# A new written-out order for five engines' queues, and one tile turned by TensorE instead of a DMA

## The chip, the cores and the metric

The kernel runs on one core of a Trainium2 chip. The metric is the device time of one execution in microseconds (us). Three runs of the kernel before took 1645.88, 1646.5 and 1651.99 us; the median is 1646.5 us. The engines are named as in the profile: PE is TensorE (PEld its weight loads), DVE is VectorE, ACT is ScalarE, POOL is GpSimd, and SP is the queue that does nothing but issue DMAs.

## The reference, cut to what matters

Four blocks with residuals run one after the other on 2048 tokens of width 512: A, B, A, B. Block A walks over 64 segments of 32 tokens, and each segment needs the memory rows that the segment before it wrote, so the 64 steps form a chain. Block B is linear attention: it sums keys times values over all tokens, and only then can any output row be computed.

```python
# A: S=2048, Dm=512, H=32 heads of Dh=128, M=8 memory rows, seg=32
for s in range(n_seg):                       # 64 steps
    h = concatenate([mem, xs], axis=1)       # 8 + 32 rows
    q, k, v = h @ Wq, h @ Wk, h @ Wv
    p = softmax(where(mask, q @ k.T * scale, -1e9))
    o = (p @ v) @ Wo
    mem = o[:, :M, :]                        # the next step's memory
    outs.append(o[:, M:, :])
# B: phi(t) = where(t > 0, t + 1, exp(t)) + 1e-6
kv, z = einsum(phi(k), v), sum(phi(k))
o = (phi(q) @ kv) / (phi(q) @ z + 1e-6) @ wo
# whole
x = x + A(layernorm(x)); x = x + B(layernorm(x))   # twice
```

## The kernel before

**Tiles and steps.** The 2048 tokens are 16 tiles of 128 rows; four steps of A use one tile. `a_layer(layer)` writes the steps `s` of one A block, with `layer` 0 or 1, and `b_in` and `b_out` of the B blocks are woven in between. Each step consists of named stages, and every operation has a key of layer, step, stage and number:

- `kq0`, `kq1`, `v`: products of the step's 32 rows (8 memory rows and 24 fresh rows) with Wk, Wq and Wv, in two halves of the heads each (L2121, L2010).
- `mem0`, `mem1`: attention of the memory rows, which the next step needs. `x`: attention of the fresh rows.
- `out`: the product with Wo (L2345) into a PSUM bank; half of it is copied to `outW`, then the DVE adds both halves into `y_sb` (L2354). `y_sb` has one slot for all steps' rows, and another for the rows named next.
- `next`: picks the memory rows out of `y_sb` by a product with `selm_sb` (L2371) and copies them into `hT`, the transposed input of the next step's `kq` and `v`.
- `res`: moves the step's other rows from `y_sb` to `dx_sb` by two DMAs, one issued by POOL and one by SP (L1909). Only when both have read `y_sb` can the next step's `out` write it.
- `left0`, `left1`, `leftv` (`left_block`): since 8 rows of a step's 32 tokens are left over, those of four steps are collected and projected together, once for each tile, by 24 groups of four matmuls with 512 columns. `prep` comes before it.
- `prep` (`prepare`): layer norm of the next tile (L2058 to L2064), then the normalised rows are transposed and copied into `hT`. For the first tile of a layer the transpose is a product on PE (L2075) into PSUM; for all others it is a DMA transpose issued by SP (`turn`, L2049) into `xT`. `xT` shares its memory with `vtmp`, which `leftv` also uses.
- `xl` loads a tile of x; in layer 1 `bo` (`b_out`) loads it from `xs_scratch` and corrects it with the B block of layer 0.
- `bi` (`b_in`): the B block's layer norm, a DMA transpose, products and running sums for one tile; it also stores x to `xs_scratch` and phi(q) to `pq_scratch`.
- At the end of layer 1: `lr` projects the last left-over rows of tile 15 and moves them by three DMAs on POOL and three on SP; `ldpq` turns all phi(q) back from `pq_scratch` by four DMA transposes on SP into the space of Wq; `ldxs` loads x; then `bi` of the last tile, `bm` (which folds kv into the output weights) and `bl`, the last B block's output tile by tile.

**What sets the order.** Nothing is scheduled at run time. The dictionary `PLACE` (L16 to L1526) gives every operation of the 1509 stages a number, in the thousandths of a microsecond in which a planner once counted. `schedule` sorts all operations by it, and this order is each engine's instruction stream; the letter `a` or `v` behind a number puts a copy on ACT or on DVE where both can do it. `finalize` adds the semaphore waits that the data need. So the numbers set only who stands behind whom in a queue: an engine that waits for a semaphore holds up all that stands behind it. The costs and latencies that `add` is given (`0.45`, `lat=3.0`) were the planner's inputs; they do not reach the chip.

**The beginning.** SP issues the loads of Wk, Wq and Wv (4 MB each), of Wo in 16 pieces and of `wqkv`, in this order, and stands still while their queue is full; the first DMA transpose comes behind them. `spin4` is a block of products of ones that keeps PE busy until Wq is there.

Of the kernel before, what the change touches and what calls it, by code (L numbers as in the profile page):

```python
# [16 lines left out]
    (0, -9, 'setup'): '1131 3371 2811 2813 9533 9534 10942 10946 10947 11056 11059 15131 15691 15692 17375 17376 19002 27477 29851 31623 38758 39985 10941 570 1130 1690 2250 2810 3370 3930 9531 9532 10940 10943 10944 10948 10949 11055 11058 11060 11061 11062 11210 11770 12330 12890 13450 14010 14570 15130 15690 17372 17371 16250 16810 17370 19001 29419a 9535 10945a 67899 17930 19000 27045 29422 32312 15133 2812 11057',  # L17
    (0, -4, 'start'): '14570v',
    (0, -2, 'left0'): '24454 24886 25965 26396 27036a 28340 28987a 29421',
    (0, -2, 'left1'): '27907 28986 29418 29850 30489a 31621 31858a 32719',  # L20
    (0, -2, 'leftv'): '34490 34922 35353 35785 36425a 37193 37636 37637a 38186 38757',
    (0, -2, 'prep'): '10138 10860 11054 12330 13451 15132 15690v 16250v 30982a 42475a 34099v',
    (0, -2, 'spin4'): '19003',
    (0, 0, 'kq0'): '25533 27044 27476 28555 29854v 32311 29853a 31622',
    (0, 0, 'kq1'): '16810 17373 17374 17377 25317 27036 28339 30489 26397v 27036 31128a 31857',
    (0, 0, 'mem0'): '31992 32718 33289 33090 33557 37080 38186 38756 38913 39315',
    (0, 0, 'mem1'): '33081 33139 34235 33557 37429 39075 39986 40103 40161 40563',
    (0, 0, 'next'): '46847 47346 47347a',
    (0, 0, 'out'): '39707 40323 42290 42396 42399 42400 42476 42477 43826v 45469',
    (0, 0, 'ql'): '29420a 32310a',  # L30
    (0, 0, 'v'): '36217 36648 37192 37636 38263a 39708a',
    (0, 0, 'x'): '33859 34234 34581 34996 35785 37080 36649v 37192v 39075v 36648v 40820 39984 40043 42397 42475 47348a 46705v 39925 40102 42291 42475 55641v 55958a',
    (0, 0, 'xl'): '0',
    (0, 1, 'kq0'): '48093 48944 50705 50706 51332a 51764 51116a 52052',
    (0, 1, 'kq1'): '47446 49173 50708 50709 48525 50707 50899 51115 52685a 53058 52627a 52628',
    (0, 1, 'mem0'): '52626 52684 53056 53175 53324 54186 54407 54808 54274 55148',
    (0, 1, 'mem1'): '53324 53424 53916 54274 54185 54809 55049 55426 54810 56136',
    (0, 1, 'next'): '58338 58392 58657a',
    (0, 1, 'out'): '55640 55698 55958 56135 56353 56571 56790 57089 57718a 57894',
    (0, 1, 'ql'): '47708v 38756v',  # L40
    (0, 1, 'res'): '66656 61715',
    (0, 1, 'v'): '51331 51763 52194 53057 53917v 53424a',
    (0, 1, 'x'): '54391 54811 55147 55639 56571 56702 56948v 56571v 57229a 57088v 57228 57658 57835 57893 58011 58338v 58908v 57717 57776 57952 58123 66655v 62145v',
    (0, 2, 'kq0'): '58907 59338 59770 60417 61714a 62350 61713v 61929',
    (0, 2, 'kq1'): '60202 61497 61712 62144 60849 61065 61281 61928 62713v 63814 62851a 63321',
    (0, 2, 'left0'): '42530 42962 43393 43825 44465a 45106 45584a 46226',
    (0, 2, 'left1'): '44465 44688 45584 45983 46704a 47345 48093a 48525',
    (0, 2, 'leftv'): '45469 46706 47349 47708 48943a 49584 50063 50062a 50704 51763',
    (0, 2, 'mem0'): '62792 63713 64246 64354 64353 64946 65215 65586 65238 65826',
# [2672 lines left out]
```

## Time and profile before

| what | value |
|---|---|
| median of three runs | 1646.5 us |
| profiled execution | 1649.09 us, span from first to last instruction 1647.0 us |
| PE busy | 1544.7 us (94%), 48837 matmuls |
| DVE, ACT, POOL busy | 1219.7, 1056.1, 191.5 us |
| mean granted clock of PE | 0.991 |
| DMA | 58.28 MB |

The span is what the instruction records cover, and the profiled execution has 2.1 us around it. A matmul here covers a quarter of the array's columns (128 rows by 32 columns); four of them run side by side, so a line with a duration of 0.39 us and x4 does not mean that PE is occupied for 0.39 us: the next such group starts about 0.22 us later. In a timeline the columns are the start in us, the duration in us, the engine, the line, the operation, the tiles written and read, and in brackets the engine's idle time before it with what ended it.

### The profile page before, as it was taken

To read this page: it belongs to the slowest core of one execution; us is meant where nothing else is said; L and a number is where in the kernel's file an instruction comes from. 1 tells how busy PE (TensorE), PEld (TensorE's weight loads), DVE (VectorE), ACT (ScalarE), POOL (GpSimd) and SP (SyncE) were. 2 spreads that over 40 slices of the span, in tenths; PEclk is the share of its full clock that TensorE was granted. 3 is DMA by queue.
4 is the path that set the end of the run, shared out by engine and by line. 5 is a ranking of instruction groups with operands and counts; after the bars stand their busy time and mean duration, and the time that the engine had idled before them with its cause. 6 is when DMAs were issued, how large, how long until landed. Compare 5 with 4: busy or idle time off the path is not lost.

```text
span 1647.0 us, 97785 instructions
## 1 busy us (share of the span) xinstructions
PE 1544.7 (94%) x48837; PEld 820.7 (50%) x40483; DVE 1219.7 (74%) x3603; ACT 1056.1 (64%) x3097; POOL 191.5 (12%) x388
## 2 busy tenths in 40 slices
PE   5799999999999998999899999999999999999987
PEld 1345545555555554554444555455555545555543
DVE  3477767777787787777677787777877777777757
ACT  2466667676766666666466675766666666766654
POOL 2011101111111101111100111011111011111010
PEclk9999999999999999999999999999999999999998
DMA  9300001001010001000000100101010111010133
GB/s 380 99 20 19 13 18 23 23 23 22 20 23 14 23 23 22 20 20 23 22 10 16 29 20 19 26 23 26 20 29 13 22 29 26 20 23 19 29 65 104
DMA packets 79892, 58.28 MB, mean 35 GB/s; under 512 B 59416, under 2 KB 74168, under 8 KB 77944
## 3 DMA queue, kind: packets, MB, share of 16 engines
q1 hardware_dynamic: 66456, 36.43, 8.5%
q0 software_dynamic: 12864, 15.46, 3.4%
q8 instruction: 351, 5.75, 1.5%
q14 instruction: 61, 0.50, 0.1%
q10 hardware_dynamic: 160, 0.14, 0.0%
HBM read 25.57 MB, written 10.35 MB: 22 GB/s over the span
## 4 chain that ended last, share of the span: by engine, by line
PE 73%; DVE 10%; DMA 8%; ACT 5%; issue 3%; SPq 1%; POOL 0%; DVEq 0%; POOLq 0%; ACTq 0%
PE pb L2121 26%; PE pb L2010 19%; PE pb L2345 14%; PE pb L2022 8%; DMA arena_sb<-arena_sb 3%; DVE arena_sb L1894 2%; ACT arena_sb L1893 2%; DMA dx_sb<-y_sb 2%; PE pb L2512 2%; DMA Wq_sb<-in_A_Wq_dram 1%; PE pb L2209 1%; DVE arena_sb L2139 1%; DVE st_sb L2058 1%; PE pb L2371 1%; DVE y_sb L2354 1%
## 5 line engine op out<-in xcount | busy, mean ns | idle before, releaser
L1893 ACT ACTIVATE arena_sb<-pb 128x512 bf16<-128x512 f32 (+3 forms) x1039 | 503.8, 511 | 300.9 <-PE pb L2010 154.7
L1894 DVE CAST arena_sb<-pb 128x512 bf16<-128x512 f32 (+3 forms) x600 | 316.9, 535 | 93.0 <-PE pb L2010 47.0
L2121 PE MATMUL pb<-Wk_sb,arena_sb 128*32 128x512 bf16 x4096 | 368.5, 381 | 5.0 <-DMA Wk_sb<-in_A_Wk_dram 2.1
L2345 PE MATMUL pb<-Wo_sb,arena_sb 128*32 128x256 bf16 x10368 | 341.5, 273 | 12.4 <-issue 8.6
L2139 DVE STREAM_TRANSPOSE arena_sb<-arena_sb 128x256 f32<-128x256 f32 x640 | 262.7, 430 | 63.7 <-ACT arena_sb L1893 58.0
L2345 PEld LDWEIGHTS pb<-Wo_sb,arena_sb 128*32 128x32 bf16 x10368 | 258.2, 96 | 56.2 <-issue 20.8
L2121 PE MATMUL pb<-Wq_sb,arena_sb 128*32 128x512 bf16 x3072 | 273.1, 382 | 11.0 <-DVE arena_sb L1894 8.4
L2022 PE MATMUL pb<-arena_sb 128*32 128x128 bf16 (+2 forms) x10800 | 264.0, 208 | 13.1 <-DVE arena_sb L1894 5.1
L1909 POOL DMA_DIRECT2D dx_sb<-y_sb x252 | 128.1, 512 | 1207.5 <-DVE y_sb L2354 829.1
L2121 PE MATMUL pb<-Wv_sb,arena_sb 128*32 128x512 bf16 x2560 | 255.5, 381 | 1.3 <-issue 1.2
L2010 PE MATMUL pb<-Wv_sb,arena_sb 128*32 128x512 bf16 x2560 | 254.9, 381 | 0.0
L2022 PEld LDWEIGHTS pb<-arena_sb 128*32 128x32 bf16 x10800 | 183.9, 95 | 136.1 <-DVE arena_sb L1894 36.9
L2121 PEld LDWEIGHTS pb<-Wk_sb,arena_sb 128*32 128x32 bf16 x4096 | 113.1, 97 | 185.0 <-issue 96.1
L2010 PE MATMUL pb<-Wq_sb,arena_sb 128*32 128x512 bf16 x2048 | 202.9, 380 | 0.0
L1893 ACT ACTIVATE arena_sb<-arena_sb 32x256 bf16<-32x256 bf16 (+2 forms) x396 | 141.2, 359 | 45.9 <-DVE arena_sb L2293 30.1
L2121 PEld LDWEIGHTS pb<-Wq_sb,arena_sb 128*32 128x32 bf16 x3072 | 86.4, 97 | 117.9 <-issue 50.3
L1894 DVE COPY arena_sb<-arena_sb 32x256 bf16<-32x256 bf16 (+2 forms) x522 | 103.1, 201 | 23.5 <-DMA arena_sb<-arena_sb 12.8
L2354 DVE TENSOR_TENSOR y_sb<-pb,outW_sb 64x256 bf16<-64x256 f32 x162 | 67.8, 419 | 65.0 <-ACT outW_sb L1893 52.7
L2257 DVE TENSOR_TENSOR arena_sb<-pb,arena_sb 128x128 bf16<-128x128 f32 x252 | 73.1, 290 | 54.2 <-ACT arena_sb L2245 22.4
L2010 PE MATMUL pb<-Wk_sb,arena_sb 128*32 128x512 bf16 x1024 | 104.1, 384 | 0.4 <-issue 0.4
L2121 PEld LDWEIGHTS pb<-Wv_sb,arena_sb 128*32 128x32 bf16 x2560 | 71.7, 96 | 65.5 <-issue 39.4
L1893 ACT ACTIVATE outW_sb<-pb 64x256 f32<-64x256 f32 x134 | 50.6, 377 | 82.5 <-PE pb L2345 78.8
(111 smaller groups left out, 1800.2 us busy)
## 6 DMA issues: line engine op xcount, KB each, us to landing
Wk_sb<-in_A_Wk_dram SPq DMA_DIRECT2D x1, 4096.0 KB, 13.3
Wq_sb<-in_A_Wq_dram SPq DMA_DIRECT2D x1, 4096.0 KB, 24.6
Wv_sb<-in_A_Wv_dram SPq DMA_DIRECT2D x1, 4096.0 KB, 34.1
Wo_sb<-in_A_Wo_dram SPq DMA_DIRECT2D x16, 256.0 KB, 7.2
xs_scratch<-x_sb POOLq DMA_DIRECT2D x32, 128.0 KB, 2.0
pq_scratch<-arena_sb POOLq DMA_DIRECT2D x31, 128.0 KB, 2.4
x_sb<-xs_scratch POOLq DMA_DIRECT2D x16, 128.0 KB, 2.9
dx_sb<-y_sb SPq DMA_DIRECT2D x126, 12.0 KB
```

Source lines behind the costliest of these rows:

```text
L1893: return e.activation(o() if callable(o) else o, i() if callable(i) else i, ACTF.Copy)
L1894: return e.tensor_copy(o() if callable(o) else o, i() if callable(i) else i)
L1909: add(eng, lambda e: e.dma_start(o, i), 0.55 if eng == "pool" else 0.4, reads=reads, writes=writes, dsem="%s%d" % (kind, k), lat=lat + (0. ...
L2010: return pe.add_instruction(mybir.InstMatmult(name=nc.get_next_instruction_name(), engine=mybir.EngineType.PE, ins=[pe.lower_ap(x), pe.low ...
L2022: r = pe.matmul(o[q], w[:, q], x, start=start, stop=stop, skip_group_check=True, tile_position=(0, 32 * j))
L2058: add("dve", lambda v: v.bn_stats(st[:, 0:6], x), c_dve(512), reads=[xk], writes=[("st", k)])
L2121: r = pe.matmul(o, blk[:, c, :], w, start=(c == 0), stop=(c == 3), tile_position=(0, 32 * j))
L2139: add("dve", lambda v: v.transpose(dst, src(img[:, k, :].bitcast(F32))), 0.445, reads=[("img", k)], writes=[dkey])
L2257: add("dve", lambda v: v.tensor_tensor(oTb[:, s % NO, 16 * b:16 * b + 16, 0:8].rearrange("p (i j) q -> p j i q", i=4), heads(pv.f32()[:, 0 ...
L2345: r = pe.matmul(tl.f32()[32 * j:32 * j + 32, 0:256], oT[:, 4 * hh + n, :], Wo_sb[:, 8 * n + hh, 256 * d:256 * d + 256], start=(hh == 0 and ...
L2354: add("dve", lambda e: e.tensor_tensor(y_sb[0:64, k, :], tl.f32()[a, 0:256], outW[c, v, :], ALU.add), c_dve(256), reads=[("outW", w)], til ...
L2512: r = pe.matmul(dst.f32()[q, :], xlnT[:, c, q], wqkv_sb[:, c, o:o + D], start=c == 0, stop=c == 3, skip_group_check=True, tile_position=(0 ...
```

## The change

All 1509 entries of `PLACE` get new numbers, so that the order of all five queues changes. Of the 2730 operations that can run on ACT or DVE, 580 go from DVE to ACT and 578 from ACT to DVE. The planner's inputs for DMAs are others (they do not reach the chip). In layer 0 the second tile (`G` = 1) is transposed by PE, as the first already was, and not by a DMA; its copies into `hT` read PSUM in place of `xT`.

```diff
 PLACE = {
...
-    (0, 0, 'out'): '39707 40323 42290 42396 42399 42400 42476 42477 43826v 45469',
-    (0, 0, 'next'): '46847 47346 47347a',
-    (0, 1, 'kq0'): '48093 48944 50705 50706 51332a 51764 51116a 52052',
-    (0, 2, 'left0'): '42530 42962 43393 43825 44465a 45106 45584a 46226',
-    (0, 2, 'left1'): '44465 44688 45584 45983 46704a 47345 48093a 48525',
-    (0, 2, 'leftv'): '45469 46706 47349 47708 48943a 49584 50063 50062a 50704 51763',
-    (0, 2, 'prep'): '9530 10939 13450 15134 26396 40323 42289v 46847v 47815v 42398a 42395v',
-    (1, 63, 'lr'): '1509542 1511104 1511279 1511497 1511716 1511934 1512211 1513000 1513332a 1513775 1516848 1516846 1516214 1516213 1515880 1516847 1520274',
-    (1, 63, 'res'): '1517060 1518203',
-    (1, 64, 'out'): '1517329 1517547 1517766 1517984 1518202 1518421 1518639 1518858 1519284a 1519798',
-    (1, 64, 'ldpq'): '1513124',
-    (1, 65, 'ldpq'): '1516273',
-    (1, 66, 'ldpq'): '1516786',
-    (1, 67, 'ldpq'): '1516845',
...
+    (0, 0, 'out'): '44931 44932 45137 45347 46599 46818 47370 47588 48015a 48443',
+    (0, 0, 'next'): '48918 48972 49238v',
+    (0, 1, 'kq0'): '50187 50188 50343 50775 52071v 53366 51639a 52502',
+    (0, 2, 'left0'): '32789 33221 38204 38917 40575a 41216 41694v 43407',
+    (0, 2, 'left1'): '31826 32258 37097 41696 44067v 45136 45626a 47588',
+    (0, 2, 'leftv'): '41218 45139 45624 46168 47588v 49345 49823 51206a 51206 51854',
+    (0, 2, 'prep'): '10030 10753 10947 11280 11535 12011 14073a 14074a 15580a 31272a 14072a',
+    (1, 63, 'lr'): '1516941 1519098 1519098 1519757 1519976 1520458 1521060 1521816 1522467a 1523228 1526143 1526276 1525536 1528233 1524158 1526119 1529184',
+    (1, 63, 'res'): '1526277 1528232',
+    (1, 64, 'out'): '1526275 1526493 1526712 1526930 1527149 1527367 1527585 1527804 1528231v 1528708',
+    (1, 64, 'ldpq'): '1524572',
+    (1, 65, 'ldpq'): '1537336',
+    (1, 66, 'ldpq'): '1538732',
+    (1, 67, 'ldpq'): '1539078',
...
 }
...
     qk_view = [W.rearrange("(c p) h e -> p c (h e)", p=128) for W in (A_Wq, A_Wk, A_Wv)]
 
     def x_move(o, i, k, reads, writes, kind, eng="pool", lat=2.0):
-        add(eng, lambda e: e.dma_start(o, i), 0.55 if eng == "pool" else 0.4, reads=reads, writes=writes,
+        add(eng, lambda e: e.dma_start(o, i), 0.55 if eng == "pool" else 0.66, reads=reads, writes=writes,
             dsem="%s%d" % (kind, k), lat=lat + (0.4 if eng == "pool" else 0.0))
 
     shift = [0]
...
 
     ln_no = [0]
 
-    def turn(o, i, reads, writes, kind, lat=3.0):
-        add("sp", lambda e: e.dma_start_transpose(o, i), 0.45, reads=reads, writes=writes, dsem=kind, lat=lat)
+    def turn(o, i, reads, writes, kind, lat=2.8):
+        add("sp", lambda e: e.dma_start_transpose(o, i), 1.2, reads=reads, writes=writes, dsem=kind, lat=lat)
 
     def layernorm(t, after=None, dst=None):
         k = ln_no[0] % 2
...
             busy = spin(layer, step, "spin", *SPIN[layer, 1]) if not first and G == 0 else None
             at(step, "prep")
             r2 = G % 2
-            tl = layernorm(G, busy, None if G == 0 else (xT, ["vtmp"], "dtx"))
+            pe_turn = G <= first
+            tl = layernorm(G, busy, None if pe_turn else (xT, ["vtmp"], "dtx"))
             if first and G == 0:
                 ready.append(spin(layer, step, "spin4", *SPIN[0, 4]))
                 ready[0].sync.add(late[0])
                 at(step, "prep")
                 P.count = 6
-            if G:
+            if not pe_turn:
                 view = xT.rearrange("p c (g x) -> p c g x", g=4)
                 src, tls, rd, sb, rate = lambda: view, [], ["vtmp"], 1, 4
             else:
...
                 b_out(1, s, t, 0)
             elif t:
                 at(s, "xl")
-                x_move(x_sb[:, slot(t), :], x_view[t], slot(t), [], [("x", slot(t))], "dxl", lat=8.5 if t == 1 else 2.0)
+                x_move(x_sb[:, slot(t), :], x_view[t], slot(t), [], [("x", slot(t))], "dxl", lat=8.5 if t == 1 else 3.0)
 
         at(-4, "start")
         evac(hT[:, 0, 0, :, 0:8], memT0_sb[:, :, :], 32, reads=["memT0"], writes=[("hTm", 0, 0)])
...
                 P.at(1, step + i // 4, "ld" + nm)
                 nd = add("sp", (lambda e, vw=vw, i=i, n=n: e.dma_start(XE[:, 1, i:i + n, :], vw[i:i + n].rearrange("t p d -> p t d")))
                          if w else (lambda e, vw=vw, i=i, n=n: e.dma_start_transpose(
-                             XQ[:, :, i:i + n, :].rearrange("p c t x -> p c (t x)"), vw[i:i + n].rearrange("t p d -> (t p) d"))), 0.6,
+                             XQ[:, :, i:i + n, :].rearrange("p c t x -> p c (t x)"), vw[i:i + n].rearrange("t p d -> (t p) d"))), 0.6 if w else 2.6,
                     reads=[(nm, t) for t in range(i, i + n)], writes=[("XE", w, t) for t in range(i, i + n)],
                     after=P.res["Wq"][1] + free, dsem="dl%s%d" % (nm, i), lat=t0 + 0.22 * i)
                 if prev is not None:
...
             else:
                 e, ek = quarters(e_sb), ["e"]
         else:
-            x_move(x, xs_view[t], k, [("xs", t)], [xk], "dxl")
+            x_move(x, xs_view[t], k, [("xs", t)], [xk], "dxl", lat=2.5)
             turn(e, pq_view[t], [("pq", t)], ek, "dtq")
         td, ty = P.tile(), P.tile()
```

2990 rows, old and new, of the table PLACE are left out of this document.

## The prediction

> **What bounds the kernel now.** I read the page first, then a table of stretches, then the waits of PE.
>
> ```profile
> span 1647.0 us, 97785 instructions
> PE 1544.7 (94%) x48837; PEld 820.7 (50%) x40483; DVE 1219.7 (74%) x3603; ACT 1056.1 (64%) x3097; POOL 191.5 (12%) x388
> ...
> PE 73%; DVE 10%; DMA 8%; ACT 5%; issue 3%; SPq 1%; POOL 0%; DVEq 0%; POOLq 0%; ACTq 0%
> ```
>
> ```profile
> 0.00:62.00 62.00, 36.77 (x665) 9.95 (x415) 18.40 (x57) 14.89 (x41) 10.92 (x42) 0.89 0.82 306
> 62.00:1600.00 1538.00, 1477.43 (x47452) 797.26 (x39404) 1171.77 (x3489) 1020.53 (x3019) 180.04 (x345) 1.00 0.10 22
> 1600.00:1647.00 47.00, 30.45 (x732) 13.45 (x664) 29.54 (x57) 20.65 (x38) 0.55 (x1) 0.88 0.37 112
> ```
>
> In the stretches the columns are the stretch, its length, the busy time of PE, PEld, DVE, ACT and POOL, the clock granted to PE, the DMA share and GB/s. PE is the bound, and the change takes no product away, so it can win only PE's idle time and the time lost at a low clock. The idle time is 62.0 - 36.8 = 25.2 us in the first 62 us, 1538.0 - 1477.4 = 60.6 us in the 1538 us that follow (4%), and 47.0 - 30.5 = 16.5 us in the last 47 us. Both ends also have a mean clock under 1. Per us the ends are the poor stretches, so I look at them by instruction and at the middle by its waits.
>
> ```profile
> PE pb L2121 <- DVE arena_sb L1894: 10.1, 9, 4.0
> PE pb L2345 <- issue: 8.6, 18, 1.0
> ...
> PE pb L2022 <- DVE y_sb L2354: 7.8, 4, 6.4
> ...
> PE pb L2371 <- DVE y_sb L2354: 6.3, 13, 2.6
> ...
> PE pb L2022 <- issue: 2.4, 5, 1.1
> ```
>
> Each row says which instruction of PE waited for whom: us in total, how often, and the longest. Two of the longest, 4.0 and 6.4 us, are single events, one at each end.
>
> **The beginning: tile 2 turned by PE.** Here are the queue of SP, the DVE, and PE.
>
> ```profile
> 2.42 39.21 SPq L1924 DMA_DIRECT2D Wo_sb<-in_A_Wo_dram  x16
> ...
> 42.40 23.53 SPq L2049 DMA_TRANSPOSE arena_sb<-arena_sb  x2
> ```
>
> ```profile
> 12.97 0.56 DVE L2064 TENSOR_SCALAR arena_sb<-x_sb,st_sb 128x512 bf16<-128x512 bf16 x1
> ...
> 52.40 0.29 DVE L1894 COPY arena_sb<-arena_sb 128x128 bf16<-128x128 bf16 x2 [6.90 <-DMA arena_sb<-arena_sb]
> 52.72 0.43 DVE L1894 COPY outW_sb<-pb 64x256 f32<-64x256 f32 x1
> ...
> 57.40 0.42 DVE L2354 TENSOR_TENSOR y_sb<-pb,outW_sb 64x256 bf16<-64x256 f32 x1
> ```
>
> ```profile
> 11.50 0.62 PE L2075 MATMUL pb<-id_sb,arena_sb 128*32 128x128 bf16 x16 [8.34 <-DVE arena_sb L2064]
> 14.18 1.90 PE L2121 MATMUL pb<-Wk_sb,arena_sb 128*32 128x512 bf16 x16 [2.06 <-DMA Wk_sb<-in_A_Wk_dram]
> ...
> 33.52 0.21 PE L2217 MATMUL pb<-arena_sb 128*32 128x64 bf16 x4 [1.28 <-DVE arena_sb L2139]
> ...
> 36.40 0.64 PE L2010 MATMUL pb<-Wv_sb,arena_sb 128*32 128x512 bf16 x4
> 36.83 0.64 PE L2121 MATMUL pb<-Wv_sb,arena_sb 128*32 128x512 bf16 x4
> ...
> 47.98 0.62 PE L2345 MATMUL pb<-Wo_sb,arena_sb 128*32 128x256 bf16 x16 [1.65 <-DMA Wo_sb<-in_A_Wo_dram]
> 52.65 0.62 PE L2121 MATMUL pb<-Wq_sb,arena_sb 128*32 128x512 bf16 x4 [4.05 <-DVE arena_sb L1894]
> ...
> 59.06 0.38 PE L2121 MATMUL pb<-Wq_sb,arena_sb 128*32 128x512 bf16 x4
> 59.28 0.38 PE L2010 MATMUL pb<-Wk_sb,arena_sb 128*32 128x512 bf16 x4
> ...
> 60.50 0.40 PE L2121 MATMUL pb<-Wk_sb,arena_sb 128*32 128x512 bf16 x4
> ```
>
> Tile 2's normalised rows are ready at 12.97 + 0.56 = 13.53 us, but their DMA transpose stands behind the sixteen Wo loads and is issued at 42.40 us; it lands at 52.4 us. Until then PE stands still for 4.05 us with `left0` at the head of its queue. What that holds up matters more: the copy to `outW` of step 0's output stands behind the waiting copies on the DVE and starts at 52.72 us although the product ended at 47.98 + 0.62 = 48.60 us; `y` follows at 57.40 us, and step 1's first `kq` product begins at 60.50 us.
>
> With the change the transpose costs the product of 16 matmuls once, 0.62 us by the row at 11.50 us. It comes ahead of the Wk product, which waits 2.06 us for its weights anyway. The rows are ready at 13.53 us, before Wk's 14.18 us, so I cost it at 0 (0.62 us if that cover is gone). The 24 groups of `left_block` then stand between 31.8 and 47.6 in the new order, ahead of `next` of step 0. They need 24 x 0.22 = 5.2 us, 0.22 us being the spacing from 59.06 to 59.28 us.
>
> ```profile
> 26.00:48.00 22.00, 16.56 (x372) 6.02 (x283) 8.07 (x27) 9.18 (x26) 0.00 (x0) 0.84 1.06 379
> ```
>
> Of these 22 us PE is idle for 5.4 us, and some 3.4 us more go to the low clock (a mean of 0.84, so 0.16 x 22), so 5.2 us of work fit. Step 0's `out` still ends at 48.6 us, when the last piece of Wo has come. From there the copy (0.43), the sum (0.42), the select and its copy (about 0.2 each) and four hand-overs lead to step 1's `kq` at some 50.2 us rather than 60.50 us: -10.3 us. The other end is the removed wait alone, -4.05 us, if the left block doesn't fit before; a loss is excluded, as no transfer is added and the rows are early. I take -9.5, close to the first end, since the queue behind the wait is seen to move with it.
>
> The low clock is a part of this. At 36.40 and 36.83 us the groups come 0.43 us apart, twice the 0.22 us, and the longest wait in the rows just before is 1.28 us. So short waits suffice for a slow stretch, one can stay in the new beginning, and I don't take the whole 10.3 us. The Trainium skill ("TensorE: Matmul & The Clock Gate", Part 1) has the clock halved only after an idle window of some 3.4 us. By that rule no slow stretch is left once the 4.05 us wait is gone, and the term is the whole -10.3; the stretch at 36.40 us doesn't agree with it.
>
> **The end: SP's queue.** The rows are those of SP, DVE and PE.
>
> ```profile
> 1595.31 7.39 SPq L2614 DMA_TRANSPOSE Wq_sb<-pq_scratch  x3
> 1602.74 2.10 SPq L1909 DMA_DIRECT2D dx_sb<-y_sb  x3
> ```
>
> ```profile
> 1597.19 0.42 DVE L2354 TENSOR_TENSOR y_sb<-pb,outW_sb 64x256 bf16<-64x256 f32 x1
> 1606.10 0.42 DVE L2354 TENSOR_TENSOR y_sb<-pb,outW_sb 64x256 bf16<-64x256 f32 x1 [8.50 <-DMA dx_sb<-y_sb]
> ```
>
> ```profile
> 1598.21 1.93 PE L2345 MATMUL pb<-Wo_sb,arena_sb 128*32 128x256 bf16 x64 [0.23 <-ACT arena_sb L1893]
> 1606.58 0.62 PE L2022 MATMUL pb<-y_sb,selz_sb 128*32 128x256 bf16 x8 [6.44 <-DVE y_sb L2354]
> ```
>
> ```profile
> dx_sb<-y_sb POOLq DMA_DIRECT2D x126, 12.0 KB, 1.9
> ```
>
> Step 63's `y` is ready at 1597.6 us, yet SP is issuing three DMA transposes for 7.39 us, and the row moves come behind them. The last step's sum can't write `y_sb` until they have read it: 1606.10 us, with PE idle for 6.44 us. In the old `PLACE` three of the four `ldpq` (1516273 to 1516845) stand ahead of `res` of step 63 (1518203); in the new one it is one (1524572 ahead of 1528232), and the other three stand behind at 1537336 to 1539078. So the move can be issued near 1598 us and lands 1.9 us later, at about 1600, when the last `out` ends too (1598.21 + 1.93 = 1600.14). With the copy, the sum comes at about 1600.6 us: -5.5 us. The three transposes that are moved back then run from 1600 to 1607.4 us on SP. Their first use is in `bl`, after the B block's own chain of some 12 us, so they are covered; if not, up to 5 us come back. I take -5.5, with -7 (a warm clock behind it) and -0.5 as ends.
>
> **The middle.** No wait here is long, and the numbers show no place, only kinds. Waits for "issue" in the two rows above make 8.6 + 2.4 = 11.0 us. The change says it orders by instruction fetches and transfer times. The Trainium skill ("Runtime: NRT & Kernel Launch", Instruction fetch mechanics) holds that fetches are mostly hidden; by that rule this term is 0 and the total 4 us higher. The 18 waits of L2345, up to 1.0 us, speak against it, though no row names the fetch as their cause. `next` waiting for `y` (6.3 us in 13) partly starts here, where the DVE stands before a tile's statistics:
>
> ```profile
> 213.57 0.69 DVE L2058 BATCH_NORM_STATS2 st_sb<-x_sb 128x6 f32<-128x512 bf16 x1 [3.79 <-DMA x_sb<-in_A_x_dram]
> ```
>
> ```profile
> L1893 ACT ACTIVATE arena_sb<-pb 128x512 bf16<-128x512 f32 (+3 forms) x1039 | 503.8, 511 | 300.9 <-PE pb L2010 154.7
> L1894 DVE CAST arena_sb<-pb 128x512 bf16<-128x512 f32 (+3 forms) x600 | 316.9, 535 | 93.0 <-PE pb L2010 47.0
> ```
>
> The copies that change engines (580 one way, 578 the other, 511 against 535 ns) leave both loads as they are: 0. A new order may take away the 11.0 and 6.3 us and the 6.1 us that the first wait row has besides the beginning's 4.0, together some 23 us. It may as well add as much, because it reshuffles every queue and any copy that comes later than planned stops PE. Between -23 and +23 I take -5, a third of the issue waits and a fifth of the `next` waits.
>
> **Sum.** -9.5 - 5.5 - 5 = -20 us. The profiled execution took 1649.1 us (span 1647.0 and 2.1 around it), 2.6 above the median of 1646.5; the same 20 us off the median give **1626.5 us**. What a measurement can tell from no change is about 0.5%, or 8.2 us, hence faster means under 1638.3 and slower over 1654.7.
>
> **The rivals.**
> - *The middle gains its full 23 us.* Then it is 1646.5 - 15 - 23 = 1608.5. For it speaks that DMA is 8% of the chain; against it that the many waits are each under 1 us and come from copies, whose costs the change leaves alone. Chance 0.17.
> - *Only waits are exchanged at the ends.* The left block doesn't fit before the Wo wait (-4) and the moved transposes hold up `bl` (-0.5): with the middle at -5, 1637. Chance 0.08.
> - *The middle gives the ends' gain back.* New waits of about 15 us: 1646.5. It is the case if the new order fits the engines no better than the old one. Chance 0.15.
> - *Slower: SP's queue holds the row moves elsewhere.* In the new order six of the 126 `res` moves on SP stand behind a tile's transpose that was behind them before (those of steps 9, 59 and 60 of layer 0 and 14, 25 and 38 of layer 1; eleven go the other way). If that transpose waits for its own input, the move waits too and the next `y` can't be written, as at the end, where it cost 6.44 us. Six times that is 39 us: 1626.5 + 39 = 1665. It decides only once the hold is longer than the slack, and a step takes 1538 / 126 = 12.2 us, of which the move needs 1.9. A transpose that is itself only a few us late does nothing. Chance 0.10.
>
> **How the numbers follow.** The forecast has 0.50. Faster takes in the forecast, the full gain, the exchange (1637), and a little of the fourth case: 0.50 + 0.17 + 0.08 + 0.02 = 0.77. The rest of the middle's giving back is no change, 0.13; slower is 0.10. The range leaves out the slower case and the far half of the full gain: 1607 to 1650.
>
> **What would show it.** Right: PE's transpose L2075 twice by 13 us; step 1's `kq` at 50 to 51 us; no wait of 4 us for L1894 there; at the end one wait under 2 us for L2354 ahead of L2022, with the three `ldpq` behind the row moves; the middle's idle time at 50 to 60 us. Wrong: PE's idle time in the middle above 75 us, DVE waiting over 10 us for `dx_sb<-y_sb` between the ends, or `left0` of tile 2 again waiting for a DMA.

## The result, and the profile after

The changed kernel takes 1626.1 us in the median of four runs (1621.9 to 1630.0), beside 1648.3 us for the kernel before (its three runs and a fourth): a ratio of 0.9863, with a 95% interval from 0.9829 to 0.9897. The whole interval lies beyond the bound of 0.5%, so it is faster, by 22 us; 20 us and 1626.5 us were forecast.

The page, two lines of it, and then the same three kinds of stretch as before (length, busy time of PE, PEld, DVE, ACT and POOL, granted clock, DMA share, GB/s). The last two rows are cut where the new last step begins.

```profile
span 1627.4 us, 97760 instructions
PE 1534.2 (94%) x48853; PEld 810.1 (50%) x40499; DVE 1226.8 (75%) x3601; ACT 1059.4 (65%) x3099; POOL 191.6 (12%) x388
```

```profile
0.00:62.00 62.00, 41.67 (x1017) 15.51 (x707) 30.09 (x88) 19.70 (x58) 11.43 (x43) 1.00 0.83 306
62.00:1590.00 1528.00, 1464.50 (x47120) 781.35 (x39128) 1166.56 (x3457) 1019.57 (x3005) 179.65 (x344) 1.00 0.10 22
1590.00:1628.00 38.00, 28.02 (x724) 13.25 (x664) 30.14 (x58) 20.15 (x36) 0.55 (x1) 0.92 0.59 151
```

PE's work is the same (16 matmuls more, those of the new transpose), but the first 62 us now hold 41.67 us of it instead of 36.77, and their clock is 1.00 instead of 0.89. PE's idle time in the middle has not fallen: it is 1528.0 - 1464.5 = 63.5 us, where it was 60.6. Here are the waits of PE by kind:

```profile
PE pb L2513 <- DMA arena_sb<-arena_sb: 14.4, 13, 1.9
PE pb L2022 <- DVE arena_sb L1894: 10.0, 28, 1.3
...
PE pb L2372 <- DVE y_sb L2355: 6.1, 20, 0.8
...
PE pb L2121 <- DVE arena_sb L1894: 4.0, 7, 1.3
...
PE pb L2346 <- issue: 3.3, 7, 1.4
PE pb L2022 <- DVE y_sb L2355: 3.3, 3, 1.4
...
PE pb L2022 <- issue: 0.9, 2, 0.6
```

Lines from about 2170 on have moved by one: L2346 is the `out` product, L2355 the sum into `y_sb`, L2372 `next`, L2513 the products of `b_in`. Both long single waits are gone (4.0 at L2121, 6.4 at L2022), and the waits for issue in the two rows quoted before fell from 11.0 to 4.2 us.

The timeline of PE at the beginning, and the DVE's sum in it:

```profile
9.64 0.61 PE L2075 MATMUL pb<-id_sb,arena_sb 128*32 128x128 bf16 x16 [2.40 <-DVE arena_sb L2064]
...
14.55 1.90 PE L2121 MATMUL pb<-Wk_sb,arena_sb 128*32 128x512 bf16 x16 [4.29 <-DMA Wk_sb<-in_A_Wk_dram]
...
36.40 0.39 PE L2121 MATMUL pb<-Wv_sb,arena_sb 128*32 128x512 bf16 x4
36.62 0.39 PE L2010 MATMUL pb<-Wv_sb,arena_sb 128*32 128x512 bf16 x4
...
47.49 0.62 PE L2346 MATMUL pb<-Wo_sb,arena_sb 128*32 128x256 bf16 x16
...
49.04 0.22 PE L2372 MATMUL pb<-selm_sb,y_sb 128*32 128x16 bf16 x8 [0.82 <-DVE y_sb L2355]
49.59 0.40 PE L2121 MATMUL pb<-Wk_sb,arena_sb 128*32 128x512 bf16 x4 [0.33 <-DVE arena_sb L1894]
```

```profile
48.57 0.42 DVE L2355 TENSOR_TENSOR y_sb<-pb,outW_sb 64x256 bf16<-64x256 f32 x1 [0.46 <-ACT outW_sb L1893]
```

The second transpose on PE is done at 10.3 us, in the wait for Wk. Step 0's sum comes 0.5 us after its product instead of 9 us after it, and step 1's `kq` starts at 49.59 us instead of 60.50. At 36.40 us the groups now stand 0.22 us apart, at full clock.

The end: the queue of SP, the DVE, PE.

```profile
1579.63 2.13 SPq L2615 DMA_TRANSPOSE Wq_sb<-pq_scratch  x1
1581.81 6.62 SPq L1909 DMA_DIRECT2D dx_sb<-y_sb  x5
1588.47 6.61 SPq L2615 DMA_TRANSPOSE Wq_sb<-pq_scratch  x3
```

```profile
1590.48 0.42 DVE L2355 TENSOR_TENSOR y_sb<-pb,outW_sb 64x256 bf16<-64x256 f32 x1 [0.47 <-DMA dx_sb<-y_sb]
```

```profile
1587.60 1.93 PE L2346 MATMUL pb<-Wo_sb,arena_sb 128*32 128x256 bf16 x64 [0.39 <-ACT arena_sb L1893]
1590.96 0.40 PE L2022 MATMUL pb<-y_sb,selz_sb 128*32 128x256 bf16 x8 [1.43 <-DVE y_sb L2355]
1591.40 2.55 PE L2010 MATMUL pb<-one_sb 128*32 128x512 bf16 x44
```

The three transposes stand behind the row moves, and the wait for the last sum is 1.43 us instead of 6.44. For the experiments I cut each span at two products that every version has: the start of step 1's first `kq`, and the start of the last `out`.

| profiled execution | start | middle (PE idle in it) | end | span |
|---|---|---|---|---|
| before | 60.5 | 1537.7 (60.6) | 48.8 | 1647.0 |
| after | 49.6 | 1538.0 (64.1) | 39.8 | 1627.4 |
| after, a second job | 50.1 | 1530.9 (58.6) | 39.7 | 1620.7 |

The two ends gave 10.9 + 9.0 = 19.9 us. The medians differ by 22.2 us, so some 2 us are left for the middle; in the second job the ratio was 0.9869 (21.5 us), the ends gave 19.5 us, and 2 us are left again. The intervals reach 4 to 6 us to either side, so these 2 us can't be told from none, nor from the 5 that were forecast. The 7 us between the two middles are a difference of two executions of one kernel. So the middle of one profile is good to about 7 us; the starts of these two agree to 0.5 us and the ends to 0.1.

### The profile page after: what moved, and what is told of

It reads as the page before. It is cut to its first block, busy times and chain, and to the rows that moved or that the text cites. A ratio compares the mean times of both kernels' runs of the same rounds, so it can differ in the third digit from the quotient of the medians.

```text
span 1627.4 us, 97760 instructions
## 1 busy us (share of the span) xinstructions
PE 1534.2 (94%) x48853; PEld 810.1 (50%) x40499; DVE 1226.8 (75%) x3601; ACT 1059.4 (65%) x3099; POOL 191.6 (12%) x388
## 3 DMA queue, kind: packets, MB, share of 16 engines
q8 instruction: 350, 5.73, 1.5%
## 4 chain that ended last, share of the span: by engine, by line
PE 68%; DVE 13%; DMA 10%; ACT 7%; issue 2%; POOL 0%; SPq 0%; DVEq 0%
PE pb L2121 25%; PE pb L2010 17%; PE pb L2346 12%; PE pb L2022 8%; DMA arena_sb<-arena_sb 5%; DVE arena_sb L1894 3%; ACT arena_sb L1893 2%; DMA dx_sb<-y_sb 2%; DMA Wv_sb<-in_A_Wv_dram 2%; DVE arena_sb L2139 2%; PE pb L2513 2%; PE pb L2210 1%; DVE y_sb L2355 1%; DVE arena_sb L2294 1%; PE pb L2372 1%
## 5 line engine op out<-in xcount | busy, mean ns | idle before, releaser
L1893 ACT ACTIVATE arena_sb<-pb 128x512 bf16<-128x512 f32 (+4 forms) x1032 | 499.6, 511 | 293.1 <-PE pb L2010 131.5
L1894 DVE CAST arena_sb<-pb 128x512 bf16<-128x512 f32 (+3 forms) x614 | 322.3, 533 | 105.7 <-PE pb L2010 64.9
L2121 PE MATMUL pb<-Wk_sb,arena_sb 128*32 128x512 bf16 x4096 | 363.3, 381 | 8.2 <-DMA Wk_sb<-in_A_Wk_dram 4.3
L2346 PE MATMUL pb<-Wo_sb,arena_sb 128*32 128x256 bf16 x10368 | 340.0, 273 | 5.7 <-issue 3.3
L2346 PEld LDWEIGHTS pb<-Wo_sb,arena_sb 128*32 128x32 bf16 x10368 | 257.7, 96 | 53.5 <-issue 15.9
L2022 PE MATMUL pb<-arena_sb 128*32 128x128 bf16 (+2 forms) x10800 | 266.6, 209 | 18.3 <-DVE arena_sb L1894 10.0
L2121 PE MATMUL pb<-Wq_sb,arena_sb 128*32 128x512 bf16 x3072 | 266.9, 379 | 3.3 <-DVE arena_sb L1894 2.8
L2022 PEld LDWEIGHTS pb<-arena_sb 128*32 128x32 bf16 x10800 | 183.5, 96 | 149.5 <-DVE arena_sb L1894 45.5
L2121 PE MATMUL pb<-Wv_sb,arena_sb 128*32 128x512 bf16 x2560 | 251.4, 378 | 2.3 <-ACT arena_sb L1893 1.2
L2010 PE MATMUL pb<-Wv_sb,arena_sb 128*32 128x512 bf16 x2560 | 251.2, 378 | 0.0
L2121 PEld LDWEIGHTS pb<-Wk_sb,arena_sb 128*32 128x32 bf16 x4096 | 110.5, 97 | 196.4 <-issue 97.3
L2010 PE MATMUL pb<-Wq_sb,arena_sb 128*32 128x512 bf16 x2048 | 200.7, 379 | 0.0
L1893 ACT ACTIVATE arena_sb<-arena_sb 32x256 bf16<-32x256 bf16 (+2 forms) x411 | 146.9, 361 | 38.8 <-DVE arena_sb L2294 29.1
L2121 PEld LDWEIGHTS pb<-Wq_sb,arena_sb 128*32 128x32 bf16 x3072 | 83.8, 96 | 93.6 <-issue 43.6
L2355 DVE TENSOR_TENSOR y_sb<-pb,outW_sb 64x256 bf16<-64x256 f32 x162 | 67.8, 419 | 55.4 <-ACT outW_sb L1893 51.3
L2121 PEld LDWEIGHTS pb<-Wv_sb,arena_sb 128*32 128x32 bf16 x2560 | 70.1, 95 | 66.1 <-issue 36.9
L2010 PE MATMUL pb<-Wk_sb,arena_sb 128*32 128x512 bf16 x1024 | 101.6, 379 | 0.0
```

Of the source, the lines that this page charges most:

```text
L1893: return e.activation(o() if callable(o) else o, i() if callable(i) else i, ACTF.Copy)
L1894: return e.tensor_copy(o() if callable(o) else o, i() if callable(i) else i)
L2010: return pe.add_instruction(mybir.InstMatmult(name=nc.get_next_instruction_name(), engine=mybir.EngineType.PE, ins=[pe.lower_ap(x), pe.low ...
L2022: r = pe.matmul(o[q], w[:, q], x, start=start, stop=stop, skip_group_check=True, tile_position=(0, 32 * j))
L2121: r = pe.matmul(o, blk[:, c, :], w, start=(c == 0), stop=(c == 3), tile_position=(0, 32 * j))
L2346: r = pe.matmul(tl.f32()[32 * j:32 * j + 32, 0:256], oT[:, 4 * hh + n, :], Wo_sb[:, 8 * n + hh, 256 * d:256 * d + 256], start=(hh == 0 and ...
```

## The experiments

In all of them the ratio is that to the kernel before in the same job, and "us less" is 1 minus the ratio, times the median before.

**1. The product alone.** The old order, and tile 2 transposed on PE; only this entry of `PLACE` differs.

```diff
-    (0, 2, 'prep'): '9530 10939 13450 15134 26396 40323 42289v 46847v 47815v 42398a 42395v',
+    (0, 2, 'prep'): '9530 10939 13450 15134 15500 15690 16805v 16806v 16807v 16808a 16809a',
...
-            tl = layernorm(G, busy, None if G == 0 else (xT, ["vtmp"], "dtx"))
+            pe_turn = G <= first
+            tl = layernorm(G, busy, None if pe_turn else (xT, ["vtmp"], "dtx"))
...
-            if G:
+            if not pe_turn:
```

> The kernel before with one thing changed: tile 2 is transposed by PE, its copies follow at once, and all else keeps the old order (left0 behind step 0's attention). Theory (the two ends carry the whole gain, the product itself most of the beginning's): PE no longer waits 4.05 us for L1894, step 1's kq begins near 53 us instead of 60.5 (the 5.2 us of the left block still come after 46 us), one slow-clock stretch is gone, and the time falls by 6 to 8 us to about 0.996 of before. Rival (the order carries the beginning): the wait is only exchanged for the one on Wo and y, kq at 56 us or later, -2 to -4 us, ratio 0.998.

Measured: 1632.4 us, ratio 0.9917 (0.9903 to 0.9932), 14 us less. `kq` of step 1 started at 53.2 us (-7.3), the end stayed at 48.6 us, and the middle of this execution was 8.0 us shorter. The first groups of the left block, before and in this run:

```profile
53.05 0.64 PE L2010 MATMUL pb<-Wk_sb,arena_sb 128*32 128x512 bf16 x4
53.47 0.64 PE L2121 MATMUL pb<-Wq_sb,arena_sb 128*32 128x512 bf16 x4
```

```profile
48.28 0.39 PE L2121 MATMUL pb<-Wq_sb,arena_sb 128*32 128x512 bf16 x4
48.49 0.39 PE L2010 MATMUL pb<-Wk_sb,arena_sb 128*32 128x512 bf16 x4
```

The 7.3 us are the wait and the slow clock behind it. Before, the left block started 4.67 us after the last part of `out`, and its first 14 groups came 0.43 us apart; here it starts 0.45 us after it, with groups some 0.22 us apart from the first on. From there to `kq` it was 7.85 us before and is 4.95 here. SP and PE at the end of this run:

```profile
1580.04 7.01 SPq L2615 DMA_TRANSPOSE Wq_sb<-pq_scratch  x3
1587.09 2.10 SPq L1909 DMA_DIRECT2D dx_sb<-y_sb  x3
```

```profile
1590.95 0.61 PE L2022 MATMUL pb<-y_sb,selz_sb 128*32 128x256 bf16 x8 [6.09 <-DVE y_sb L2355]
```

So the product gives most of the beginning without the new order, and leaves the end's wait as it was. The 8 us in the middle were not expected (the forecast was 6 to 8 us in all). With them PE's waits for issue fell from 14.9 us in 31 to 8.3 in 18, although the order is the old one; runs 5 to 9 come back to this.

**2. The DMA transpose back, in the new order.** The changed kernel, with tile 2 turned by a DMA again, and its copies and left block near their old places (`leftv` 1.5 us later). So this run undoes the product and the new place of the left block together.

```diff
-    (0, 2, 'left0'): '32789 33221 38204 38917 40575a 41216 41694v 43407',
-    (0, 2, 'left1'): '31826 32258 37097 41696 44067v 45136 45626a 47588',
-    (0, 2, 'leftv'): '41218 45139 45624 46168 47588v 49345 49823 51206a 51206 51854',
+    (0, 2, 'left0'): '42530 42962 43393 43825 44465a 45106 45584a 46226',
+    (0, 2, 'left1'): '44465 44688 45584 45983 46704a 47345 48093a 48525',
+    (0, 2, 'leftv'): '46969 48206 48849 49208 50443a 51084 51563 51562a 52204 53263',
...
-    (0, 2, 'prep'): '10030 10753 10947 11280 11535 12011 14073a 14074a 15580a 31272a 14072a',
+    (0, 2, 'prep'): '10030 10753 10947 11280 11535 42400 42500v 46847v 47815v 42510a 42505v',
...
-            pe_turn = G <= first
+            pe_turn = G == 0
```

> The changed kernel with tile 2 transposed by a DMA again, and its left block back at the old numbers (leftv 1.5 later, as the banks need it); all else is the new order. Theory: the DMA again lands at 52 us behind the weights, PE waits some 4 us, kq of step 1 at 59 to 61 us instead of 49.6, and the time is 9 to 11 us over the changed kernel's (ratio to before about 0.993). Rival (the new order absorbs a late tile): kq at 53 us or earlier, +3 us.

Measured: 1638.5 us, ratio 0.9966 (0.995 to 0.9983). PE's timeline:

```profile
47.52 0.62 PE L2121 MATMUL pb<-Wq_sb,arena_sb 128*32 128x512 bf16 x4 [6.10 <-DVE arena_sb L1894]
...
58.53 0.40 PE L2121 MATMUL pb<-Wk_sb,arena_sb 128*32 128x512 bf16 x4
```

The wait for the DMA's copies is back (6.10 us), `kq` starts 8.9 us later than after, and the end keeps its gain (40.6 us). From here to the changed kernel are 0.0097 to 0.0103, 16 to 17 us, more than the 9 to 11 expected: 9 us of them are the beginning, the rest lies in the middle (1544.3 us here, in an execution 6.6 us over this kernel's median), where one profile is only good to some 7.

**3. The transposes in front of the row moves, in the new order.** The other half undone. The moves of step 63 and of the last rows are put behind the last transpose, and the sum behind them (their entries `lr` and `out` are not shown).

```diff
-    (1, 63, 'res'): '1526277 1528232',
+    (1, 63, 'res'): '1526277 1528800',
...
-    (1, 65, 'ldpq'): '1537336',
+    (1, 65, 'ldpq'): '1526000',
-    (1, 66, 'ldpq'): '1538732',
+    (1, 66, 'ldpq'): '1526001',
-    (1, 67, 'ldpq'): '1539078',
+    (1, 67, 'ldpq'): '1528750',
```

> The changed kernel with the loads of phi(q) put back ahead of the last row moves on SP (two ahead of lr's moves, the third ahead of step 63's). Theory: y of the last step waits for the move again, PE idle 5 to 6.5 us ahead of L2022 with selz, the clock falls behind it, and the end (from the last out to the end of the span) goes from 39.8 us back towards 48.8 us: +6 to +9 us. Rival (the transposes are needed early and the wait is covered by bl): +0 to +2 us.

Measured: 1625.5 us, ratio 0.9876 (0.986 to 0.9892). PE at the end:

```profile
1585.90 0.62 PE L2022 MATMUL pb<-y_sb,selz_sb 128*32 128x256 bf16 x8 [6.64 <-DVE y_sb L2355]
...
1586.72 3.67 PE L2010 MATMUL pb<-one_sb 128*32 128x512 bf16 x44
```

By the profile the mechanism is there: the wait is 6.64 us again, and the stretch from the last `out` to the end is 45.1 us, 5.3 more than after. The total does not show it: 6 to 9 us more than the changed kernel were expected, and the interval holds the changed kernel's ratios (0.9863, 0.9869). This execution's middle was short (1527.6 us), 10.5 and 3.4 us under the two of the changed kernel; why, this run doesn't show. Run 4 tests the same three transposes in the old order, where the total does show them.

**4. Both small edits in the old order.** Run 1, with three more entries changed:

```diff
-    (1, 65, 'ldpq'): '1516273',
+    (1, 65, 'ldpq'): '1518269',
-    (1, 66, 'ldpq'): '1516786',
+    (1, 66, 'ldpq'): '1518270',
-    (1, 67, 'ldpq'): '1516845',
+    (1, 67, 'ldpq'): '1518271',
```

> The kernel before with two things changed: the product of e1, and three of the four phi(q) loads moved on SP behind step 63's row move. 1500 numbers stay old. Theory (the middle gives nothing): -14 to -18 us, ratio about 0.990, and the stretch from step 1's kq to the last out stays at 1537.7 us. Rival (the middle's new order is worth 5 us or more, hidden by the spread of the profiled run): e4 stays 5 us or more over the changed kernel's time after the difference at the beginning is taken off.

Measured: 1625.1 us, ratio 0.987 (0.9852 to 0.9888), 21 us less. Against run 1 that is 7.7 us, and its end is 41.1 us where run 1's is 48.6: total and profile agree on the three transposes. Four entries of `PLACE` and the switch of `pe_turn` come out at the ratio of 1509 new entries, though not by the same way: against the kernel before, the beginning is 6.2 us shorter here and the end 7.6 (13.9 in all, where the changed kernel has 19.9), and the other 7 us lie in this execution's middle (1527.8 us), under the old order. PE's timeline, and the stretch from 26 to 48 us of this kernel:

```profile
33.36 0.21 PE L2218 MATMUL pb<-arena_sb 128*32 128x64 bf16 x4 [1.28 <-DVE arena_sb L2139]
...
36.50 0.65 PE L2010 MATMUL pb<-Wv_sb,arena_sb 128*32 128x512 bf16 x4
36.93 0.65 PE L2121 MATMUL pb<-Wv_sb,arena_sb 128*32 128x512 bf16 x4
...
47.96 0.62 PE L2346 MATMUL pb<-Wo_sb,arena_sb 128*32 128x256 bf16 x16 [1.54 <-DMA Wo_sb<-in_A_Wo_dram]
...
1584.89 0.40 PE L2022 MATMUL pb<-y_sb,selz_sb 128*32 128x256 bf16 x8 [0.93 <-DVE y_sb L2355]
```

```profile
26.00:48.00 22.00, 16.50 (x372) 5.96 (x280) 8.06 (x27) 9.33 (x27) 0.00 (x0) 0.84 1.06 378
```

Here the slow stretch at 36.50 us is left and part of the left block still stands behind Wo, so `kq` starts at 54.3 us. The new order's own gain at the beginning is the difference to its 49.6 us, 4.7 us (3.6 against run 1's 53.2 us, with the same beginning).

**5 and 6. The same orders with 32 more weight loads.** One number of `spin4`'s products changes: 32 of its products load their weights anew. They lie in PE's wait for Wq and cost no time there; all of PE's instructions behind them move by 32 places. Run 5 does it to the kernel before, run 6 to the changed one.

```diff
-    SPIN = {(0, 0): (24, 256, 72), (1, 0): (12,), (1, 1): (22, 256, 84), (0, 2): (5,), (0, 3): (7,), (0, 4): (30, 512, 10)}
+    SPIN = {(0, 0): (24, 256, 72), (1, 0): (12,), (1, 1): (22, 256, 84), (0, 2): (5,), (0, 3): (7,), (0, 4): (30, 512, 42)}
```

> The kernel before, with 32 weight loads more among the products of ones that fill the wait for Wq (spin4's third number 42 in place of 10). No order changes and the added loads lie in idle time, but all later instructions of PE stand 32 places further on in its stream. Theory (the middle's time hangs on where in the stream the waits for issue fall, as e1's middle of 1530 us under the old order suggests): the middle changes by 3 us or more either way and PE's waits for issue change from 14.9 us; the time is off before by 3 to 8 us, more likely faster. Rival (e1's and e4's shorter middle comes from the product or from the chip's spread): the time is within 2 us of before.

Measured: 1636.0 us, ratio 0.9964 (0.9947 to 0.9982), 6 us less with not one operation in another order. PE's waits for issue at `out` were 8.6 us in 18 before, and here:

```profile
PE pb L2345 <- issue: 3.2, 7, 0.9
```

> The changed kernel with the same 32 weight loads more. Theory of e5: the middle changes by 3 us or more. Rival: within 2 us of the changed kernel in the same call.

Measured: 1619.6 us, ratio 0.9858 (0.9834 to 0.9882): not to be told from run 7, the changed kernel in the same job (0.9869), as the rival had it. Its waits for issue were low without the shift and stayed so (4.8 us in 12 over all rows, against 5.9 in 13).

**7. The changed kernel again**, unaltered.

> The changed kernel once more, unaltered, beside e6 and e8 on one chip, to place it against e3 and e4 (0.9876 and 0.987 of before) by the ratio. If the middle of 1538.6 us in its first profile was one execution's, it is about 1620 to 1623 us here, ratio 0.986 or less, and its middle 1528 to 1535; if it belongs to the order, the middle is again 1536 or more and the ratio that of e3 in spite of an end that is 5.3 us shorter.

Measured: 1622.4 us, ratio 0.9869 (0.9846 to 0.9892). Its waits of `b_in` for the transpose are lower than in the first profile (14.4 in 13), so a part of those belonged to that execution:

```profile
PE pb L2513 <- DMA arena_sb<-arena_sb: 10.7, 11, 1.6
```

**8. `b_in` later.** My theory was that the new middle loses at `b_in`, whose products stand too early behind their DMA transposes. So in the changed kernel the operations of `bi` from the eighth on got 1500 added, 1.5 us later in the planner's count, for 13 tiles. One of them:

```diff
-    (0, 18, 'bi'): '232674 233397 234316 234374 234932 237896 234315 238041 238689 239444 246539 247259 248071 249019 251209a 251434 251032 251803 251497 250051 252010 254301 260712',
+    (0, 18, 'bi'): '232674 233397 234316 234374 234932 237896 234315 239541 240189 240944 248039 248759 249571 250519 252709a 252934 252532 253303 252997 251551 253510 255801 262212',
```

> The changed kernel with the products and what follows of b_in 1.5 us later in the order for 13 of the 30 tiles where the banks allow it (steps 18, 26, 34, 50, 54 and 58 of layer 0 and 6, 14, 22, 30, 34, 38 and 50 of layer 1). Theory (the waits of L2513 for its DMA transpose, 14.4 us in 13, are what the new middle pays for its shorter waits for issue): these waits fall by a third or more and the time by 2 to 5 us. Rival (what is moved only waits elsewhere): within 1.5 us of the changed kernel.

Measured: 1651.0 us, ratio 1.0052 (1.0033 to 1.0071), slower than the kernel before. The waits of PE:

```profile
PE pb L2372 <- DVE y_sb L2355: 15.6, 29, 1.1
...
PE pb L2513 <- DMA arena_sb<-arena_sb: 7.7, 9, 1.4
```

The waits aimed at fell (10.7 to 7.7 us), and those of `next` for `y` rose from 6.1 to 15.6 us, which I put down to `b_in`'s copies now standing in front of the chain's sums; no run tests that. The middle was 1560.4 us with 79.0 us idle, 20 more than in run 7 with 58.6. Its length grew by 29.5 us; the other 9 us show in no wait but as more busy time of PE for the same products (1481.5 us against 1472.3), and why stays open. The theory fell: here an order is only good as a whole.

**9 to 11. More shifts.** Run 9 is run 4 with the 32 loads of run 5; run 10 is the kernel before with 64 loads more (74 in place of 10), run 11 the changed kernel with 64.

> The old order with the two small edits of both ends, and 32 more weight loads in the idle wait for Wq. If the two effects are of different places (the ends about -19 us, the place in PE's instruction stream where waits for issue fall about -5), they add up: ratio about 0.983, some 1617 us, and this order beats the changed kernel. If the shift only helps the unaltered old stream, and the two edits of the ends have shifted the later stream already, it is within 3 us of what the two edits gave alone: ratio 0.986 to 0.989.

> The kernel before with 64 more weight loads instead of 32. If the middle depends on where the instruction fetches fall, the waits for issue come out at a third value, anywhere between 5 and 16 us, and the time follows them: ratio between 0.994 and 1.002. If the 32 loads helped in another way (more loads of any number help), 64 give the same or more: waits for issue near 6 us in some 13 and ratio 0.996 or less.

> The changed kernel with 64 more weight loads. If its order was planned for the fetches as they fall, any shift away from them should cost: waits for issue above 8 us and 3 to 8 us more than the changed kernel (ratio 0.989 to 0.992). If the plan does not catch the fetches, it stays within 3 us of the changed kernel (ratio 0.985 to 0.988), as with 32 loads.

PE's waits for issue at `out`, in run 9, in run 10 and in run 11:

```profile
PE pb L2346 <- issue: 8.2, 23, 0.7
```

```profile
PE pb L2345 <- issue: 8.2, 23, 0.9
```

```profile
PE pb L2346 <- issue: 5.5, 14, 0.7
```

| order | loads added | waits for issue, all rows of PE | ratio |
|---|---|---|---|
| before | 0 | 14.9 us in 31 | 1 |
| before | 64 | 13.0 us in 35 | 0.9994 (0.9981 to 1.0007) |
| before | 32 | 6.1 us in 13 | 0.9964 (0.9947 to 0.9982) |
| before with both edits | 32 | 12.0 us in 34 | 0.9905 (0.9885 to 0.9925) |
| before with both edits | 0 | 8.6 us in 19 | 0.987 (0.9852 to 0.9888) |
| changed | 64 | 8.1 us in 21 | 0.990 (0.9876 to 0.9923) |
| changed | 0 | 4.9 us in 11; 5.9 in 13 | 0.9863 (0.9829 to 0.9897); 0.9869 (0.9846 to 0.9892) |
| changed | 32 | 4.8 us in 12 | 0.9858 (0.9834 to 0.9882) |

Run 9 missed what I had put down for both cases: the loads that help the old stream by 6 us cost the same stream with two edits some 6 us (0.0035, across two jobs, and the two intervals just touch). Run 10 came out at the third value that the dependence on place asks for, and gives nothing; so more loads don't by themselves help. Run 11 came out as its first case said (8.1 us of waits, 0.990), but run 6 had not, so it isn't shown that the new order was fitted to one place. In each order more waits for issue go with more time: 6.9 us of them with 5 us between the shifts by 64 and by 32 of the first order, 3.4 with 6 in the second, 2 to 3 with 5 to 6 in the third (there at the edge of the intervals). Shown is that loads which cost nothing where they stand, and move only the place of PE's later instructions in their stream, are worth some 6 us in the old order; a loss of the same size in the second order is likely. Runs 1 and 4 add instructions of PE, too, so their shorter middles need not come from their edits; of run 4's 21 us, run 9 kept 16. That the waits are for instructions that a DMA has yet to bring is argued: the page of the changed kernel lists such transfers, the line below, 5.73 MB / 350 = 16.4 KB each, but no row ties a wait to one of them.

```profile
q8 instruction: 350, 5.73, 1.5%
```

No version beat the changed kernel beyond the intervals.

## Why the prediction was right, and where not

**The total** was forecast as -20 us and came out at -22. It is right for the reasons given at both ends, and a little by luck: both end terms were too small, by 1.4 and 3.5 us, and the middle gave, as far as the medians tell, some 3 us less than it was to give.

**The beginning, -9.5, measured -10.9** (-10.4 in the second job). The steps held: the product L2075 a second time by 10.3 us, no wait of 4 us for the copies, step 0's sum right behind its product, `kq` at 49.6 to 50.1 us where 50 to 51 was said. Run 1 changes the turn alone and shows that the DMA was the cause and gives 7.3 of it; in run 2 the DMA brings the wait back. That the rest goes with the left block's earlier place is read from the timelines of runs 1 and 4. The far end of my range, -4.05 for the removed wait alone, left out the slow groups behind that wait, which run 1 has at 2.9 us. That SP stands still because the queue of loads is full is inferred from the 39.21 us that its sixteen issues take; no row names it.

I had not taken the whole 10.3 us because a slow stretch could stay. In the changed kernel none did: the clock granted from 26 to 48 us was 1.00. In run 4 it was 0.84, as before, with groups 0.43 us apart at 36.50 us. The wait of 4 us had no part in that stretch, since it comes 12 us later. How full PE is doesn't decide it either. The first row is that of the changed kernel, the second that of run 10, which has the old order and less busy time:

```profile
26.00:48.00 22.00, 18.59 (x475) 7.38 (x332) 13.41 (x38) 9.58 (x27) 0.00 (x0) 1.00 1.06 378
```

```profile
26.00:48.00 22.00, 13.94 (x376) 5.62 (x282) 8.06 (x27) 9.03 (x26) 0.00 (x0) 0.99 1.06 378
```

Run 10 has the order, the 1.28 us wait and the products of the kernel before, and no slow stretch at 36 us; run 9 has none there either. The clock records of the traces show what differs. In all thirteen profiled executions the clock changes on a fixed grid of 3.41 us (every slow stretch that ends inside the trace lasts one, two or three times that), and where this grid lies against the program differs from execution to execution. The clock fell behind 33 windows of this grid, in which PE was busy for at most 0.53 of the time; it stayed full behind some 6000, in which PE was busy for at least 0.45. Here is the window ahead of the slow stretch in the kernel before (34.76 to 41.58 us, at a clock of 0.50), 1.66 of 3.42 us busy, and then the two of run 10 over the same products, 1.76 and 2.21 of 3.41:

```profile
31.34:34.76 3.42, 1.66 (x60) 0.59 (x44) 1.88 (x6) 2.35 (x9) 0.00 (x0) 1.00 1.02 398
```

```profile
30.35:33.76 3.41, 1.76 (x36) 0.42 (x16) 2.18 (x8) 2.63 (x7) 0.00 (x0) 1.00 0.99 403
33.76:37.17 3.41, 2.21 (x68) 0.90 (x56) 1.60 (x7) 1.66 (x7) 0.00 (x0) 1.00 1.09 356
```

So waits of 1.28 and 0.44 us in one window suffice, and how the windows fall on them is chance. The 0.8 us that I took off were not the price of such a stretch: the last part of step 0's `out` starts at 48.0 us with it (before) and at 47.7 without it (run 10), as it waits for the last piece of Wo in both.

By the rule of the Trainium skill ("TensorE: Matmul & The Clock Gate", Part 1), under which an idle window of some 3.4 us halves the clock, the term would be -10.3, and -10.4 to -10.9 came. The length of the window agrees with the traces; but the windows ahead of the stretch at 36 us were not idle throughout (PE was busy for 1.66 of 3.42 us before), so my reading of the rule as one long wait was too narrow.

**The end, -5.5, measured -9.0.** The queue's step held: three transposes behind the moves, the wait at 1.43 us, and `bl` not held up. Run 4 against run 1 gives 7.5 us by the profile and 7.7 by the time. What was mis-sized is what lies behind the wait: the clock, which I had only as the far end of -7, and the B block's chain, to which I had given nothing. From the start of the last `out` to that of the product with `selz` it is 8.4 us before and 3.4 after, 5.0 less. From there to the end it is 40.4 and 36.4 us, another 4.0 less: the products of ones that follow took 4.68 us before, behind a wait of 6.44 us, and 2.55 us after. In run 3, behind 6.64 us, they took 3.67 us.

```profile
1607.40 4.68 PE L2010 MATMUL pb<-one_sb 128*32 128x512 bf16 x44
```

The line is that of the kernel before. The rows show 2.1 of these 4.0 us. The other 1.9 us lie behind the B block's own transpose on PE (L2075), from which it is 35.1 us to the end before and 33.2 after. They aren't the clock behind this wait: in run 4, where the wait is gone under the old order, it is 35.1 us again. There the parts are 5.5 us of wait, which is my term, 2.1 of clock and nothing else. So the 1.9 us came with the new order, and not in each of its executions: runs 6 and 11 have 34.8 and 35.0 us there.

**The middle, -5, about -2 left over by the medians.** The waits for issue did fall, by 6.8 us in the two rows where I had expected a third of 11.0. But those of `next` stayed (6.3 to 6.1 us), and other waits rose: those of L2022 for the copies from 6.1 to 10.0 us (9.1 to 10.7 in every run of the new order, 4.7 to 7.2 in every run of the old one), those of `b_in` for its transposes from 8.2 to 14.4 and 10.7 us (though 7.2 and 5.7 in runs 6 and 11). The step that failed is the fifth of the `next` waits, and that no row was given to what the new order would add. That the new order gains anything in the middle isn't shown: the profiles have 1527.6 to 1544.3 us with it, run 8 aside, and 1525.1 to 1537.7 with the old one. The rival in which the middle gains its full 23 us was far off; the rival in which SP holds row moves did not come: the sum waits for them once, for the 0.47 us shown above, against 8.50 before.

The fetch rule of the Trainium skill ("Runtime: NRT & Kernel Launch", Instruction fetch mechanics: fetches are mostly hidden) puts the issue part of this term at 0 and so the middle at -1, close to the 2 us left over, but not for its reason: the waits for issue did fall by 6.8 us, and other waits took the gain back. Nor are they nothing, as run 5 took 6 us off by a shift alone.

**PE's idle time in the middle** was to be 50 to 60 us; it was 63.5 and, cut at the products, 64.1 and 58.6. The mark was finer than two executions of one kernel agree.

## What to carry to other kernels

Look first at the ends of a schedule: one DMA behind sixteen loads, and three behind which a buffer is to be freed, were worth some 14 us at the two ends with four changed entries and a switch, of the 20 us that the whole new order gained there. The total of that small edit was 21 us less in one place of the stream and 16 in another, so its middle was partly luck. A wait at an end costs more than its length where the clock behind it is low, so price what follows it too. Before you credit a new order in a stream as long as this with a few us, shift the old one by some instructions in idle time and see how far that alone moves it.

## What was unexpected in the hardware

- Thirty-two weight loads in idle time moved the whole kernel by -6 us in one order and by some +6 us in another (there the two intervals just touch); 64 moved the first by nothing.
- The same kernel's middle was 1538.0 us in one profiled execution and 1530.9 in another, with waits for issue of 4.9 and 5.9 us, so these are not what differs; 5.5 of the 7 us are idle time of PE, 3.7 of them `b_in`'s wait for its transposes.
- The clock of PE fell to half for one to three windows of 3.41 us wherever PE had been busy for less than about half (0.45 to 0.53) of the window before, without any long wait: in the same order the stretch at 36 us was slow in two executions and not in a third (run 10), as the windows lay.
- Adding 1.5 us in the planner's count to part of the operations of one stage in 13 tiles cost 29 us (run 8 against run 7).
